# Attention before two MoE layers: the diagonal blocks of P turned in full 128x128 transpositions, the first queries' scores on 128 columns, and POOL's constants moved behind the scan

## The chip, the cores and the metric

One core of a Trainium2 chip runs the whole program. The metric is the device time of one execution in microseconds (us); lower is better. Engines are named as in the profile: PE (TensorE, matrix products; PEld is its weight load), DVE (VectorE), ACT (ScalarE), POOL (GpSimd), SP (SyncE, which here issues the DMAs). L170 is line 170 of the kernel before. A difference of 0.5% of the time (3.7 us) is about what a measurement of this kernel can tell from no change.

## The reference

Causal attention with a forgetting bias over 4 batches, 8 heads, 576 positions and 64 dimensions, then two dense layers on the 2304 x 512 result. The change touches the attention alone.

```python
def _attn_ref(q, k, v, s):                       # q, k, v: (4, 8, 576, 64); s: (4, 8, 576)
    scores = scale * np.matmul(q, k.transpose(0, 1, 3, 2))
    causal = np.triu(np.ones((S, S), dtype=bool), k=1)
    cum = np.cumsum(np.maximum(s, 0.0), axis=-1)
    bias = -(cum[:, :, :, None] - cum[:, :, None, :])
    scores = np.where(causal, -1000000000.0, scores + np.minimum(bias, 0.0))
    ...
    attn = np.exp(scores - max); attn = attn / (sum + 1e-09)
    return np.matmul(attn, v)

def reference(...):
    x = attn_out.transpose(0, 2, 1, 3).reshape(B * S, H * D)
    x = _moe_ref(x)      # (x @ w1) * (x @ w2) @ w3 @ w_out
    return _moe2_ref(x)  # x @ w_in, softmax-gated, layer-normed, @ w_out
```

## The kernel before

**Queries in five tiles.** A head's 576 queries are cut into five tiles `QT`: four of 128 rows that begin at 64, 192, 320 and 448 (tile `i` = 1 to 4, with 64 + 128 i keys: 192, 320, 448, 576), and one of the first 64 queries with 64 keys (`i` = 0). Tiles with the most keys come first. So the last 64 keys of each tile are its diagonal block, of which only the lower 64 queries see anything.

**One head, in stages.** `qk_part` makes the scores on PE: for heads 0 to 7 as full float32 products (L170, two passes each, so that one product is two weight loads and two matmuls in the trace), for heads 8 to 31 as two products of split words (L178 and L179). The tile of 576 keys is written as two halves of 288 columns into two PSUM banks. `softmax_tile` adds the mask and takes the maximum on DVE (L192), and the exponential on ACT (L196), into an SBUF tile `P`, where the five query tiles lie side by side at the offsets `QOF`. `normalise` scales the rows of P (two tiles on ACT at L231, three on DVE at L233).

**Turning P.** The product with V needs P with the keys on the partitions. `tr_part` transposes P on PE in four parts, two heads behind the scores: ten 128x128 blocks (L265), then the five diagonal blocks of 64x64: that of the first queries (L267) and the lower halves of the four others (L274), which come from partitions 64 to 127 of P. Each part has its own PSUM tile `tr`; its columns are copied to `PT` by ACT and DVE in turn (`evict`; L95 on ACT, L97 on DVE), seven copies for a head.

**av.** `av_parts` multiplies PT with V for a pair of heads at once (L298): each head's result takes 64 of the 128 output partitions, so these products are 128x64 in the array, and the two heads' lie beside each other. For head pairs up to head 9 this stands directly behind the second head's transpositions, afterwards one step later, behind those of the next head.

**Fill.** While the batches 1 to 3 are in attention, products of the first dense layer of the batch before (`ab_unit`, L326, names `a` and `b`, 12 products of 288 columns each) are put between the stages. `pump` converts weights that were loaded into `stage` (L363 on ACT, L369 to L374 on DVE). After the attention (345 us) come the rest of the dense layers; the change leaves them alone.

**Order.** The order in which each engine's instructions stand is made by a scheduler when the program is built, from the order in the code and its own estimate of durations. Each engine works through its own in that order.

**Start.** PE runs eight products of zeros (`zp`, L485, 16 matmuls). s is loaded, clipped by DVE (L504) and summed by a scan (L505) into `cum`; DMAs put `cum` into a row of q and of k (`QKN`, L148 and L149), and the first scores follow. POOL writes the constants: zeros and ones for the extra rows of q and k (`aug_rows`), the mask, and zeros for the upper halves of PT and VT (L527 to L532).

## Time and profile before

| what | value |
|---|---|
| median of 3 runs | 738.74 us (738.39 to 741.12) |
| the profiled execution, its own time | 737.73 us |
| its span in the trace | 736.0 us |
| PE busy in the span | 716.7 us |
| DVE, ACT, POOL busy | 504.9, 468.0, 99.5 us |
| attention, from the first scores to the last av | 8.7 to 345 us |

The busy time of PE counts a matmul from its start to its modelled end, so neighbours overlap; the time that one really takes in a row of its kind is the distance from its start to the next one's start. Where PE stands still, the profile shows idle time and what ended it.

### The profile page before, as it was taken

To read this page: it belongs to the slowest core of one execution; us is meant where nothing else is said; L and a number is where in the kernel's file an instruction comes from. 1 tells how busy PE (TensorE), PEld (TensorE's weight loads), DVE (VectorE), ACT (ScalarE), POOL (GpSimd) and SP (SyncE) were. 2 spreads that over 40 slices of the span, in tenths; PEclk is the share of its full clock that TensorE was granted. 3 is DMA by queue.
4 is the path that set the end of the run, shared out by engine and by line. 5 is a ranking of instruction groups with operands and counts; after the bars stand their busy time and mean duration, and the time that the engine had idled before them with its cause. 6 is when DMAs were issued, how large, how long until landed. Compare 5 with 4: busy or idle time off the path is not lost.

```text
span 736.0 us, 13040 instructions
## 1 busy us (share of the span) xinstructions
PE 716.7 (97%) x4682; PEld 625.0 (85%) x4682; DVE 504.9 (69%) x1267; ACT 468.0 (64%) x985; POOL 99.5 (14%) x102
## 2 busy tenths in 40 slices
PE   9889998999999999999998999999999999999997
PEld 6567978888888899899997889988888988888886
DVE  7987978897678888632887876576747365563651
ACT  4987777898766777732544745577646465564652
POOL 5033313142221331000000000001000000000000
PEclk9999999999999999999999999999999999999999
DMA  4644554655476665614566943253234142304221
GB/s 109 186 126 99 174 161 142 194 144 130 127 221 186 182 188 149 208 61 147 170 215 202 355 149 101 58 110 75 79 82 101 44 123 75 89 12 75 44 57 44
DMA packets 79829, 95.52 MB, mean 130 GB/s; under 512 B 41418, under 2 KB 52682, under 8 KB 79764
## 3 DMA queue, kind: packets, MB, share of 16 engines
q1 hardware_dynamic: 79764, 94.69, 45.0%
q8 instruction: 37, 0.61, 0.3%
q14 instruction: 28, 0.23, 0.1%
HBM read 59.04 MB, written 20.14 MB: 108 GB/s over the span
## 4 chain that ended last, share of the span: by engine, by line
PE 73%; DVE 11%; DMA 8%; ACT 5%; issue 2%; POOL 1%; SPq 0%; ACTq 0%; DVEq 0%; POOLq 0%
PE x L721 14%; PE o L847 13%; PE b L326 10%; PE a L326 10%; PE hX L753 5%; DMA stage<-in_w_dram 5%; PE av L298 4%; PE hZ L753 3%; PE tr L265 3%; ACT P L196 2%; PE sc L170 2%; PE sc L178 2%; DVE P L192 2%; DVE stage L374 2%; PE hW L753 2%
## 5 line engine op out<-in xcount | busy, mean ns | idle before, releaser
L196 ACT ACTIVATE P<-P,STAT 128x576 f32<-128x576 f32 (+4 forms) x160 | 88.3, 554 | 31.5 <-DVE STAT L192 30.9
L100 POOL TENSOR_TENSOR QK<-qk,QK 64x1152 fp32r<-64x1152 f32 x24 | 67.1, 2798 | 167.2 <-ACT QK L95 158.9
L721 PE MATMUL x<-gl,MH 128*128 128x256 f32 x288 | 80.4, 280 | 0.0
L721 PE MATMUL x<-gh,ML 128*128 128x256 f32 x288 | 80.2, 279 | 0.0
L721 PE MATMUL x<-gh,MH 128*128 128x256 f32 x288 | 79.9, 280 | 0.0
L192 DVE CUSTOM_DVE_ANT_0 P<-sc,wmask 128x576 f32<-128x576 f32 (+4 forms) x160 | 70.6, 478 | 4.5 <-PE sc L170 3.2
L326 PE MATMUL a<-xT0h,W 128*128 128x288 f32 x256 | 58.1, 300 | 1.9 <-ACT a_sb L338 1.9
L326 PE MATMUL b<-xT0h,W 128*128 128x288 f32 x256 | 57.6, 299 | 1.5 <-DVE STAT L192 0.8
L847 PE MATMUL o<-OH,lh 128*128 128x512 f32 x144 | 57.1, 397 | 0.2 <-DVE ll L100 0.2
L326 PE MATMUL a<-xT1h,W 128*128 128x288 f32 x256 | 57.2, 298 | 0.0
L847 PE MATMUL o<-OH,ll 128*128 128x512 f32 x144 | 57.0, 396 | 0.0
L847 PE MATMUL o<-OL,lh 128*128 128x512 f32 x144 | 57.0, 396 | 0.0
L326 PE MATMUL b<-xT1h,W 128*128 128x288 f32 x256 | 56.5, 295 | 0.0
L721 PEld LDWEIGHTS x<-gl,MH 128*128 128x128 f32 x288 | 54.2, 188 | 1.3
L817 DVE COPY lt<-turned 128x2048 uint16<-128x2048 uint16 x16 | 21.9, 1368 | 48.4 <-DMA turned<-half 48.4
L721 PEld LDWEIGHTS x<-gh,MH 128*128 128x128 f32 x288 | 54.0, 188 | 1.1
L721 PEld LDWEIGHTS x<-gh,ML 128*128 128x128 f32 x288 | 54.1, 188 | 0.9
L346 DVE TENSOR_TENSOR g_sb<-b,a_sb 128x288 f32<-128x288 f32 x64 | 28.8, 449 | 32.8 <-PE b L326 16.7
L363 ACT ACTIVATE stage<-stage 128x512 f32<-128x512 f32 x56 | 36.9, 674 | 21.2 <-DMA stage<-in_w_dram 18.0
L298 PE MATMUL av<-PT,VT 128*64 128x64 f32 (+4 forms) x384 | 50.1, 395 | 0.0
L231 ACT ACTIVATE P<-P,STAT 128x576 f32<-128x576 f32 x64 | 42.7, 717 | 10.4 <-DVE STAT L226 10.4
L338 ACT ACTIVATE a_sb<-a 128x288 f32<-128x288 f32 x64 | 25.6, 401 | 33.3 <-PE a L326 33.1
(193 smaller groups left out, 1965.5 us busy)
## 6 DMA issues: line engine op xcount, KB each, us to landing
stage<-in_w_dram SPq DMA_DIRECT2D x32, 512.0 KB
g_scr<-g_sb SPq DMA_DIRECT2D x32, 288.0 KB
stage<-in_wo_dram SPq DMA_DIRECT2D x16, 512.0 KB
qk<-in_qk_dram SPq DMA_DIRECT2D x24, 288.0 KB
QK<-QK SPq DMA_DIRECT2D x24, 288.0 KB
gl<-g_scr SPq DMA_DIRECT2D x24, 256.0 KB
wf<-wf_scr SPq DMA_DIRECT2D x22, 256.0 KB
out_dram<-o SPq DMA_DIRECT2D x18, 256.0 KB
```

The source lines that it names most:

```text
L100: eng.tensor_tensor(out=dst, in0=src, in1=hi_.bitcast(F32), op=ALU.subtract)
L192: mx = nc.vector.tensor_tensor_reduce(out=dst2, in0=ps_in, in1=msk, scale=-SCALE, scalar=BIG, op0=ALU.add, op1=ALU.min, accum_out=st[0:row ...
L196: ex = nc.scalar.activation(out=dst, in_=dst, func=AF.Exp, bias=st[0:rows, ti:ti + 1], scale=-1.0, accum_out=st[0:rows, 5 + ti:6 + ti],)
L231: nc.scalar.activation(out=dst, in_=dst, func=AF.Copy, scale=r)
L298: nc.tensor.matmul(st["ps"][64 * e:64 * e + 64, 448 + c0:448 + c1], vr[:, j, e], PT[(2 * p + e) % 4][:, o + c0:o + c1], **kw,)
L326: nc.tensor.matmul(ps, w_[:, c, fs], x_[:, c, sl], start=(c == 0 and w_ is WH and x_ is XH), stop=(c == KC - 1 and w_ is WL),)
L338: ab_last[0] = nc.scalar.activation(out=a_sb, in_=ps, func=AF.Copy).ins
L346: ab_last[1] = nc.vector.tensor_tensor(out=g[:, sl], in0=ps, in1=st["a"], op=ALU.mult).ins
L363: nc.scalar.activation(out=high.bitcast(F32), in_=high.bitcast(F32), func=AF.Copy, scale=2.0 ** -112)
L721: last = nc.tensor.matmul(ps[:, a], w_[:, k, m * 128:m * 128 + 128], g_[:, k % 2], start=(k == 0 and w_ is MH and g_ is GH), stop=(k == KF ...
L753: last_h[0] = nc.tensor.matmul(ps, x_[:, k], w_[:, k], start=first and k == 0 and x_ is XH and w_ is WH, stop=k == 1 and x_ is XL, skip_gr ...
L847: nc.tensor.matmul(ps, l_[:, k], w_[:, k], start=(k == 0 and l_ is LH and w_ is OH), stop=(k == KF - 1 and l_ is LL),)
```

## The change

- **P's columns** lie in the order of the tiles 2, 3, 1, 4, 0, and the tile of 576 keys has its last 64 keys in front (its scores are one product of 512 columns and one of 64, in place of two of 288). So a window of 128 columns that begins with the diagonal block of tile 2, 3 or 1 ends in the first 64 columns of the next tile.
- **Transpositions**: the five of 64x64 are replaced by three of 128x128 on such windows. The first queries' normalised block is written by `normalise` into the masked upper half of tile 1's diagonal block, and the diagonal block of tile 4 lies behind it: one transposition turns these three (with tile 1's own) at once. All thirteen of a head are now of one shape.
- **Copies to PT**: six for a head in place of seven; the last two are one of 64 partitions x 3 x 64 on DVE and one of 128x128 on ACT. DVE and ACT now take the same ones for every head. The last one holds the first queries' block, from which the first product of av is made.
- **First queries' scores** use 128 columns of q as the stationary side in place of 64 (the upper 64 rows of the result are not read).
- **V's last 64 rows** lie on partitions 64 to 127 in place of 0 to 63.
- **Constants**: a second mask `lmask` for the tile of 576 keys; the scan's zeros are `wmask`; ACT writes the ones (`const_rows`), DVE the zeros of head 1's extra rows; POOL's constants for STAT, PT and VT are issued behind the mask's diagonal, which waits for the scan.

```diff
-    QT = []
-    off = 0
-    for i in range(4, 0, -1):
-        QT.append((64 + 128 * (i - 1), 128, 64 + 128 * i, off))
-        off += 64 + 128 * i
...
+    QOF = {}
+    PW = 0
+    for i in (2, 3, 1, 4, 0):
+        QOF[i] = PW
+        PW += 64 + 128 * i
+    QT = [(64 + 128 * (i - 1), 128, 64 + 128 * i, QOF[i]) for i in range(4, 0, -1)] + [(0, 64, 64, QOF[0])]
...
     def qk_mm(h, ps_view, ti):
-        q0, rows, n, _ = QT[ti]
+        q0 = QT[ti][0]
+        rows = 128
...
         if part == 0:
-            ps = bigtile("sc")
-            qk_mm(h, [(0, ps[:, 0, 0:HS]), (HS, ps[:, 1, 0:HS])], 0)
-            softmax_tile(h, 0, ps[:, :, 0:HS], cut=2)
+            ps = flat(bigtile("sc"))
+            qk_mm(h, [(0, ps[:, 512:1024]), (512, ps[:, 448:512])], 0)
+            softmax_tile(h, 0, ps[:, 448:1024])
             return
...
         for ti, (q0, rows, n, o) in enumerate(QT):
-            dst = p_t[h][0:rows, o:o + n]
+            src = dst = p_t[h][0:rows, o:o + n]
+            if ti == 4:
+                dst = p_t[h][0:rows, QOF[1] + 128:QOF[1] + 192]
...
+    WINS = (
+        [QOF[i] for i in (1, 2, 3)] + [QOF[4] + 64],
+        [QOF[2] + 128, QOF[3] + 128, QOF[4] + 192, QOF[4] + 448],
+        [QOF[3] + 256, QOF[4] + 320],
+        [QOF[2] + 256, QOF[3] + 384, QOF[1] + 128],
+    )
...
-        if part == 2:
-            nc.tensor.transpose(ps[0:64, 256:320], pt[0:64, QOF[0]:QOF[0] + 64], ident[0:64, 0:64])
...
-            for i in range(1, 5):
-                last_tr[0] = nc.tensor.transpose(
-                    ps[0:64, 64 * i:64 * i + 64],
-                    pt[64:128, QOF[i] + 128 * i:QOF[i] + 128 * i + 64],
-                    ident[64:128, 64:128],
-                )
-            for j in (1, 3):
-                src = ps[0:64, 64 * j:64 * j + 128].rearrange("p (a b) -> p a b", a=2)
-                evict(lambda t: half_view(t, j), src)
+        for n, o in enumerate(WINS[part]):
+            last_tr[0] = nc.tensor.transpose(ps[:, 128 * n:128 * n + 128], pt[:, o:o + 128], ident)
...
+            thirds = [x.rearrange("p (a b) -> p a b", b=w) for x, w in ((PT_[0:64, 0:960], 320), (ps[0:64, 0:384], 128))]
+            evict(thirds[0][:, :, 0:64], thirds[1][:, :, 64:128])
+            evict(PT_[:, H0:H0 + 128], ps[:, 256:384])
             p_t.pop(h)
...
         def mm(j, c0, c1, **kw):
-            o = KO[j] - 128 * j
+            o = KO[j] - 128 * j if c1 > 64 else H0
...
-    nc.gpsimd.memset(zero, 0.0)
+    nc.gpsimd.memset(wmask, 0.0)
...
-    for i in range(2):
-        aug_rows(QN[i], KN[i])
+    for i, eng in enumerate((nc.gpsimd, nc.vector)):
+        eng.memset(QN[i][0:64], 0.0)
+        eng.memset(KN[i][0:64], 0.0)
+        const_rows(QN[i], KN[i])
+    nc.gpsimd.memset(lmask, 0.0)
     nc.vector.tensor_scalar(out=s_sb, in0=s_sb, scalar1=0.0, scalar2=1.0 / SCALE, op0=ALU.max, op1=ALU.mult)
-    nc.vector.tensor_tensor_scan(out=cum, data0=s_sb, data1=zero, initial=0.0, op0=ALU.add, op1=ALU.add)
+    nc.vector.tensor_tensor_scan(out=cum, data0=s_sb, data1=wmask[0:NH], initial=0.0, op0=ALU.add, op1=ALU.add)
...
+    behind_scan = tc.issue_after(diagonal.ins)
+    behind_scan.__enter__()
     for st in STAT:
         nc.gpsimd.memset(st, 1.0)
     for t in PT:
-        for j in range(5):
+        for j in (2, 3, 1):
             nc.gpsimd.memset(t[64:128, KO[j]:KO[j] + 64], 0.0)
```

**On PE, in the attention of the later heads.** Here the transpositions of one head (`tr`) stand between fill products (`b`, L326) and the scores of another head's tile of 576 keys (`sc`). Before:

```order
L326 MATMUL b<-xT0h,W_124 128x288
L265 MATMUL tr<-ident,P 128x128 x10
L267 MATMUL tr<-ident,P 64x64
L274 MATMUL tr<-ident,P 64x64 x4
L178 MATMUL sc<-QK_615 128x288
L179 MATMUL sc<-QK_615 128x288
L178 MATMUL sc<-QK_615 128x288
L179 MATMUL sc<-QK_615 128x288
```

and in the changed kernel:

```order
L303 MATMUL b<-xT0h,W_125 128x288
L247 MATMUL tr<-ident,P 128x128 x13
L177 MATMUL sc<-QK_595 128x512
L178 MATMUL sc<-QK_595 128x512
L177 MATMUL sc<-QK_595 128x64
L178 MATMUL sc<-QK_595 128x64
L303 MATMUL a<-xT0h,W_122 128x288
```

Fifteen transpositions of two shapes have become thirteen of one, and the four score products of 288 columns are two of 512 and two of 64. Every other head's transpositions are followed by av in place of scores, before as after. Over the whole program av stands on PE in 24 unbroken runs before and in 20 now. Of the 32 heads' small transpositions before, 10 had av directly behind them; now av stands 17 times directly behind a transposition of 128x128, where it did so 7 times.

**On PE, the scores of the four smaller tiles of a later head.** Before:

```order
L178 MATMUL sc<-QK_679 128x448
L179 MATMUL sc<-QK_679 128x448
L178 MATMUL sc<-QK_679 64x64
L179 MATMUL sc<-QK_679 64x64
L178 MATMUL sc<-QK_679 128x320
L179 MATMUL sc<-QK_679 128x320
L178 MATMUL sc<-QK_679 128x192
```

and now:

```order
L177 MATMUL sc<-QK_595 128x448
L178 MATMUL sc<-QK_595 128x448
L177 MATMUL sc<-QK_595 128x64
L178 MATMUL sc<-QK_595 128x64
L177 MATMUL sc<-QK_595 128x320
L178 MATMUL sc<-QK_595 128x320
L177 MATMUL sc<-QK_595 128x192
```

The order is the same; the two products of the first queries write 128 rows in place of 64.

**On POOL, at the start**, up to the constants of PT (`s_zero` holds s and the scan's zeros, `QKN` q and k with their extra rows). Before:

```order
masks.py:199 AFFINE_SELECT ident<-ident 128x128
L521 MEMSET wmask 128x576
L497 MEMSET QKN_110 64x576
L498 MEMSET QKN_110 64x576
L527 MEMSET STAT_115 128x16
...
L530 MEMSET PT_111 64x64 x4
L499 MEMSET QKN_109 2x576
L500 MEMSET QKN_109 2x576
L530 MEMSET PT_111 64x64
L522 AFFINE_SELECT wmask<-wmask 128x128
```

and now:

```order
masks.py:199 AFFINE_SELECT ident<-ident 128x128
L489 MEMSET lmask 128x576
L506 AFFINE_SELECT wmask<-wmask 128x128
L515 MEMSET STAT_116 128x16
...
L518 MEMSET PT_112 64x64 x3
```

Between the identity and the mask's diagonal, which now waits for the scan, one memset of 128x576 is left.

## Rows read from the trace of the kernel before

**Rows 1.** Page, chain that ended last: shares of the span by engine.

```profile
PE 73%; DVE 11%; DMA 8%; ACT 5%; issue 2%; POOL 1%; SPq 0%; ACTq 0%; DVEq 0%; POOLq 0%
```

**Rows 2.** Windows of the attention: length, then busy time (and count) by engine.

```profile
core 0: us, PE busy (x) PEld busy (x) DVE busy (x) ACT busy (x) POOL busy (x), PEclk, DMA share, GB/s
9.00:66.00 57.00, 51.94 (x308) 34.99 (x308) 47.60 (x172) 48.00 (x136) 11.32 (x28) 1.00 0.52 140
66.00:158.00 92.00, 86.99 (x658) 77.59 (x654) 79.08 (x228) 75.64 (x185) 25.94 (x9) 1.00 0.55 161
158.00:285.00 127.00, 126.72 (x996) 114.09 (x996) 100.29 (x297) 96.46 (x245) 33.32 (x13) 1.00 0.62 176
285.00:345.00 60.00, 58.80 (x463) 52.75 (x462) 29.40 (x83) 30.23 (x77) 2.55 (x1) 1.00 0.34 107
```

**Rows 3.** Chain that ended last, 9 to 66 us: shares by line.

```profile
by line: PE sc L170 26.0%; PE av L298 17.8%; ACT P L196 16.4%; PE tr L265 10.4%; ACT P L231 5.9%; ACT QK L95 4.1%; ACT PT L95 3.3%; DVE P L192 2.5%; issue 2.2%; PE sc L178 1.8%; DVE W L100 1.7%; PE tr L274 1.5%; PE sc L179 1.4%; DVE P L233 
```

**Rows 4.** Timeline and chain of the start: start us, length us, what.

```profile
1.24 7.19 PE L485 MATMUL zp<-zz 128*128 128x288 f32 x16 [1.24 <-DVE zz L482]
2.66 2.00 DVE L504 TENSOR_SCALAR s_zero<-s_zero 32x576 f32<-32x576 f32 x1 [1.47 <-DMA s_zero<-in_s_dram]
4.78 1.34 DVE L505 TENSOR_TENSOR_SCAN cum<-s_zero 32x576 f32<-32x576 f32 x1
6.86 1.67 DMA QKN<-cum
8.66 0.48 PE L170 MATMUL sc<-QKN 128*128 128x288 f32 x1 [0.23 <-DMA QKN<-cum]
```

**Rows 5.** Timeline of PE: one head's transpositions, scores of another behind them.

```profile
219.69 1.25 PE L265 MATMUL tr<-ident,P 128*128 128x128 f32 x10
220.88 0.24 PE L267 MATMUL tr<-ident,P 64*64 64x64 f32 x1
220.88 0.41 PE L274 MATMUL tr<-ident,P 64*64 64x64 f32 x4
221.22 0.40 PE L178 MATMUL sc<-QK 128*128 128x288 f32 x1
221.46 0.29 PE L179 MATMUL sc<-QK 128*128 128x288 f32 x1
```

**Rows 6.** Timeline of PE: transpositions with av behind them, in two places.

```profile
207.23 1.26 PE L265 MATMUL tr<-ident,P 128*128 128x128 f32 x10
...
208.75 0.28 PE L298 MATMUL av<-PT,VT 128*64 128x64 f32 x2
...
24.93 0.49 PE L265 MATMUL tr<-ident,P 128*128 128x128 f32 x3
25.35 0.27 PE L298 MATMUL av<-PT,VT 128*64 128x64 f32 x1
```

**Rows 7.** Timeline of PE: scores of the later heads.

```profile
215.11 0.37 PE L179 MATMUL sc<-QK 128*128 128x448 f32 x1
215.32 0.19 PE L178 MATMUL sc<-QK 128*64 128x64 f32 x1
215.63 0.31 PE L179 MATMUL sc<-QK 128*128 128x320 f32 x1
215.78 0.25 PE L178 MATMUL sc<-QK 128*128 128x192 f32 x1
215.98 0.32 PE L178 MATMUL sc<-QK 128*128 128x288 f32 x1
216.53 0.29 PE L326 MATMUL a<-xT1h,W 128*128 128x288 f32 x1
```

**Rows 8.** Timeline of PE: scores of the first heads, in float32.

```profile
14.82 3.21 PE L170 MATMUL sc<-qk 128*128 128x288 f32 x12
...
17.86 0.49 PE L265 MATMUL tr<-ident,P 128*128 128x128 f32 x3
18.19 1.14 PE L170 MATMUL sc<-QKN 128*128 128x288 f32 x4
19.16 0.27 PE L265 MATMUL tr<-ident,P 128*128 128x128 f32 x1
```

**Rows 9.** Groups of DVE by form: count, busy us, mean ns, idle before.

```profile
L97 DVE COPY PT<-tr 64x64 f32<-64x64 f32 x16 | 3.3, 206 | 1.2 <-ACT PT L95 1.2
```

**Rows 10.** Waits of PE, 9 to 158 us: us in total, times, longest.

```profile
PE tr L265 <- ACT PT L95: 1.1, 1, 1.1
```

More of the change, by code (lines that the diff above doesn't have):

```diff
@@ L108, in tile_attention_moe @@
     wmask = at.tile([128, S], F32, name="wmask")
+    lmask = at.tile([128, S], F32, name="lmask")
     QK = {}
-    KO = [0]
-    for j in range(5):
-        KO.append(KO[-1] + S - 128 * j)
+    KO = {2: 0, 3: 320, 4: 576, 1: 640, 0: 1024}
+    H0 = 512
     QKN = [at.tile([128, 4, S], F32, tag="QK", bufs=2, name=f"QKN{i}") for i in range(2)]
@@ L116, in tile_attention_moe @@
     KN = [t[:, 1] for t in QKN]
-    PT = [at.tile([128, KO[5]], F32, name=f"PT{i}") for i in range(4)]
+    PT = [at.tile([128, 1600], F32, name=f"PT{i}") for i in range(4)]
     STAT = [at.tile([128, 16], F32, name=f"STAT{i}") for i in range(PB)]
@@ L143, in load_v @@
         )
-        nc.sync.dma_start(out=vr[0:64, 4].rearrange("p e d -> p (e d)"), in_=vE[b, hp])
+        nc.sync.dma_start(out=vr[64:128, 4].rearrange("p e d -> p (e d)"), in_=vE[b, hp])
     def load_aug(h, src):
@@ L185, in softmax_tile @@
         dst = pt[0:rows, o:o + n]
-        msk = wmask[0:rows, S - n:S] if rows == 128 else wmask[0:rows, S - 128:S - 64]
-        if cut:
-            dst2 = dst.rearrange("p (a b) -> p a b", a=cut)
-            msk = msk.rearrange("p (a b) -> p a b", a=cut)
-        else:
-            dst2 = dst
+        msk = lmask if ti == 0 else wmask[:, S - n:S] if rows == 128 else wmask[0:rows, S - 128:S - 64]
         mx = nc.vector.tensor_tensor_reduce(
-            out=dst2, in0=ps_in, in1=msk, scale=-SCALE, scalar=BIG,
+            out=dst, in0=ps_in, in1=msk, scale=-SCALE, scalar=BIG,
             op0=ALU.add, op1=ALU.min, accum_out=st[0:rows, ti:ti + 1],
@@ L215, in qk_part @@
             q0, rows, n, _ = QT[ti]
-            view = ps[0:rows, o:o + n]
-            qk_mm(h, [(0, view)], ti)
-            views.append((ti, view))
+            qk_mm(h, [(0, ps[:, o:o + n])], ti)
+            views.append((ti, ps[0:rows, o:o + n]))
             o += n
@@ L512, in tile_attention_moe @@
     nc.vector.memset(qk3[0:64], 0.0)
-    nc.vector.memset(qk3[0:2, 0], 1.0)
-    nc.vector.memset(qk3[32:34, 1], -1.0)
+    const_rows(QN[2], KN[2])
     load_head(2)
@@ L520, in tile_attention_moe @@
     nc.sync.dma_start(out=cum_scr.bitcast(F32), in_=CK.bitcast(F32))
-    nc.gpsimd.memset(wmask, 0.0)
-    nc.gpsimd.affine_select(
+    diagonal = nc.gpsimd.affine_select(
         out=wmask[:, S - 128:S], in_=wmask[:, S - 128:S], pattern=[[-1, 128]],
@@ L528, in tile_attention_moe @@
     for t in PT:
-        for j in range(5):
+        for j in (2, 3, 1):
             nc.gpsimd.memset(t[64:128, KO[j]:KO[j] + 64], 0.0)
     for t in VT:
-        nc.gpsimd.memset(t[64:128, 4], 0.0)
+        nc.gpsimd.memset(t[0:64, 4], 0.0)
+    behind_scan.__exit__(None, None, None)
     nc.sync.dma_start(out=gln, in_=g_ln.rearrange("(k p) -> p k", p=128))
```

47 lines of the change are left out of this document (17 added, 30 removed).

## The prediction

> **What bounds the kernel now.** I read the chain that ended last first: PE holds 73% of the span [rows 1], so what counts is the time that PE's instructions take from start to start, and where PE stands still. The windows of the attention show the second: PE is busy for all but 5.1 us of 9 to 66, 5.0 us of 66 to 158, 0.3 us of 158 to 285 and 1.2 us of 285 to 345 [rows 2]. So there are two kinds of stretches. From 158 us on PE alone sets the end, and each nanosecond that PE gains or loses there counts in full. Before 158 us DVE and ACT are busy for 82 to 86% too, and in 9 to 66 the lines of PE hold some 59% of the chain (26.0 + 17.8 + 10.4 and the three small ones), ACT most of the rest [rows 3]. There PE's gains count in part: I take 60%.
>
> **The change part by part.** Starts are used for durations, since a matmul's shown length overlaps the next one's.
>
> *Transpositions.* A 128x128 one takes (1.25 - 0.27)/9 = 0.109 us from start to start (ten in 1.25 [rows 5], one alone 0.27 [rows 8]). Where scores follow, the fifteen take from 219.69 to 221.22, and the first score product behind them takes 0.24 to its successor [rows 5] in place of (216.53 - 215.98)/4 = 0.137 [rows 7]; that is 1.53 + 0.10 = 1.63. Only 10 x 0.109 + 5 x 0.06 = 1.39 of it is work by the steps within each kind ((0.41 - 0.24)/3 = 0.06 for a small one); the remaining 0.24 lies where the shape changes. Thirteen of one shape are 13 x 0.109 = 1.42: 0.21 less. Where av follows, the fifteen take 208.75 - 207.23 = 1.52 [rows 6]. av is of another shape itself, so the change of shape stays: from the third full transposition (24.93 + 2 x 0.109 = 25.15) to av directly behind it at 25.35 is 0.20 [rows 6]. Then 12 x 0.109 + 0.20 = 1.51, which is 0.01 less. By the order, 22 heads are of the first kind and 10 of the second: -4.7 us. av also stands in 4 runs fewer; entering costs 0.20 - 0.11 = 0.09 and leaving up to 0.2, so up to 1.2 us more, of which I take half. Sum -5.3 us (bounds -4.7 and -5.9). Of this, 5.75 pairs of heads at 0.22 lie in 158 to 285 (-1.3), six heads in 285 to 345 (-0.9), and -3.1 before 158 us, about -2.0 of it in 9 to 66, where av is broken up most.
>
> *Scores of heads 0 to 7* (float32). The tile of 576 keys takes 19.16 - 18.19 = 0.97 for four passes of 288 columns [rows 8], 0.84 ns a column. Two passes of 512 are 0.86, and two of 64 columns can't be faster than their weight loads of 128 columns, 0.109 each as in the transpositions: 1.08, or +0.11. The other four tiles take 17.86 - 14.82 - 0.97 = 2.07 [rows 8]; their 960 columns in two passes are 1.62 of it, and 0.45 goes to the two passes of the 64x64 product and the change of shape around them. With 128 columns of q there is no other shape, and 0.22 is left: -0.23. Net -0.12 for each of 8 heads, -1.0 us.
>
> *Scores of heads 8 to 31* (split words). Four products of 288 take 0.55 [rows 7]. Now there are two of 512, 0.21 x 512/448 = 0.24 each after the one of 448 [rows 7], and two of 64 columns with a full weight load, which the trace doesn't hold. From above, two full loads, 0.22; from below, one load hidden behind the 512, 0.11. The nearest row is that of the two products of 192, 0.20 [rows 7], which are also shorter than a weight load; I take 0.20. So 0.68 in place of 0.55, +0.13. In the first queries' tile the pair of 64x64 and the first product of 320 take 215.63 - 215.32 = 0.31, with a change of shape in it; now 0.20 + 0.15 = 0.35, +0.04. Net +0.17 for each of 24 heads, +4.1 us (bounds: -0.01 and +0.21 a head, -0.2 to +5.0 us). By stretches that is 8, 12 and 4 heads: +1.4, +2.0, +0.7. So PE's sum is -1.0 - 2.0 = -3.0 in 9 to 66, +0.3 in 66 to 158, +0.7 in 158 to 285 and -0.2 in 285 to 345.
>
> *The start.* The first scores waited for the DMA of `cum`, which landed at 8.53 [rows 4] and is issued when the scan is through, 6.12. The scan waited for L504, which took 2.00 us, longer than the scan itself (1.34) over the same 32x576 [rows 4], while POOL was writing constants. In the changed order POOL has one memset left there. If L504 then ends a microsecond earlier, PE gains less than that: the last of the 16 products of zeros starts at 1.24 + 7.19 - 0.41 = 8.02 and takes 0.24, so the scores start at 8.27 at the earliest in place of 8.66. Bounds 0 and -0.4; I take -0.4, since 2.00 us is out of line with the scan. The Trainium skill (SBUF — State Buffer, section Who interferes with whom) says that VectorE in its two-port mode and GpSimd take a shared pair of ports one at a time, and that the second blocks for a whole instruction. By that rule L504 ends soon after the last early memset, and the term is -0.4; without it the term may be 0, and the sum 0.4 higher.
>
> *Copies, masks, constants.* One copy to PT fewer for each head, the shortest of which takes 0.21 on DVE [rows 9], shared by DVE and ACT: 0.1 us per head each at most. It counts only where these engines are on the chain, 16 heads before 158 us at 40%: -0.3 (bounds 0 and -0.6). The ones on ACT and the zeros on DVE at the start cost nothing: both engines wait for the scan's input or the first scores there (DVE idle 1.47 before L504 [rows 4]). Without that cover, or if DVE's two memsets outlast its 1.47 us, the scan comes as much later, and PE has only the 0.4 us to lose before its first scores do too. The SP queue gets no DMA more; the offset of V's last rows costs nothing.
>
> *Sum.* -0.4 (start) - 3.0 x 60% = -1.8 (9 to 66) + 0.2 (66 to 158, of +0.3) + 0.7 - 0.2 - 0.3 = -1.8 us. The profiled execution took 737.73, 1.0 less than the median; it would come to 735.9. Against the median, 738.74 - 1.8 = 736.9; I say 736.7, as two of the three runs before and the profiled one lie at the lower end.
>
> **The rivals.**
>
> 1. *PE's gain counts in full, and some idle time goes.* PE is idle for 10 us before 158 us [rows 2], behind ACT and DVE. With one shape of transposition the order has fewer broken runs. If all of -3.0 counts and 2 us of the idle time go: 738.74 - 0.4 - 3.0 + 0.3 + 0.5 - 0.6 - 2.0 = 733.5. For it: 59% of the chain in 9 to 66 is PE's already. Against it: ACT is busy for 48 of 57 us there.
> 2. *The gain is lost.* ACT, DVE and the weights' DMAs keep the pace before 158 us, and the start gives nothing, since the scan's input or the DMA is what is late. Then +0.5 us of PE's later stretches and some of the copies are left: 738.9.
> 3. *av waits for the last copy.* av's first product reads the first queries' block, which is now in the head's last copy, always on ACT. For heads 0 to 9 av stands directly behind the transpositions. If ACT is late by 1.1 us as once before [rows 10], five pairs cost 5.5 us: 742.2, slower. It decides from 0.4 us a pair. Against it: one such wait in 149 us, and the scheduler can put other products between.
> 4. *The small shapes were cheap.* If the gaps around the 64x64 transpositions were not the shapes' doing, five at 0.06 would be traded for three at 0.109: +0.03 for each of 32 heads, and no gain from shapes in the scores of heads 0 to 7. The sum is then +1.0 + 4.1 + 0.9 - 0.7 = +5.3, 744. The gaps in two places speak against it [rows 5, 6]. The Trainium skill (TensorEngine Tiling, section Theoretical Speedup) gives small matrices up to twice the rate in small tiles, which is this rival; its section Key Properties says that a change of tiling mode drains the engine, and by that the trace agrees.
>
> **How the numbers follow.** Forecast 0.52 (735 to 738.3), rival 1 0.23, rival 2 0.17, rival 3 0.05, rival 4 0.03. The time is the forecast's, 736.7. The range, 733.2 to 739.6, takes in rivals 1 and 2 for the most part; below it lies the part of rival 1 in which more idle time goes, about 0.1, above it rivals 3 and 4. The bounds of the scores alone (-4.3 and +0.9) and of the start (+0.4) stay within it. 0.5% of 738.74 is 3.7 us, so faster means below 735.0: rival 1 and a few of the forecast's, 0.27. Slower means above 742.4: 0.06. The same: 0.67.
>
> **What the profile will show.** Thirteen transpositions at 0.109 and the next fill or score product without the 0.24; two products of 64 columns taking 0.20 together in the split scores; the first scores at 8.3; L490 well under 2 us; a period of two heads after 158 us longer by 0.1 us, and the attention's first 66 us shorter by some 2 us. If the pair of 64 takes 0.1, the steady stretch is shorter than before and I am too high by 4 us; if the first stretch's idle time grows by as much as PE saves, I am too low by 2.

## The result, and the profile after

The changed kernel took 731.75 us (median of 6 runs, 730.61 to 732.8) against 739.3 us (6 runs, 738.39 to 741.12): a ratio of 0.9897, 95% interval 0.9875 to 0.992. That is 7.6 us or 1.03% faster, and below the range. The profiled execution of after took 732.8 us, the highest of its six, that of before 737.73, the lowest of its six. So the two traces differ by 4.9 us only, and 2.6 us of the difference between the medians is in neither trace.

The chain that ended last, shares of the span by engine [rows 1]:

```profile
PE 81%; DVE 9%; DMA 5%; ACT 2%; issue 2%; SPq 0%; DVEq 0%; ACTq 0%
```

The windows of the attention [rows 2]:

```profile
core 0: us, PE busy (x) PEld busy (x) DVE busy (x) ACT busy (x) POOL busy (x), PEclk, DMA share, GB/s
9.00:66.00 57.00, 53.53 (x333) 40.24 (x332) 50.23 (x179) 53.45 (x147) 12.31 (x11) 1.00 0.56 149
66.00:158.00 92.00, 86.66 (x622) 79.80 (x620) 79.77 (x219) 73.16 (x179) 23.65 (x8) 0.96 0.56 163
158.00:285.00 127.00, 127.00 (x969) 116.06 (x969) 100.23 (x284) 94.70 (x233) 34.45 (x13) 1.00 0.60 171
285.00:345.00 60.00, 60.00 (x463) 55.03 (x462) 29.49 (x82) 28.77 (x71) 0.15 (x1) 1.00 0.36 129
```

PE's idle time fell from 5.1 to 3.5 us in 9 to 66 and from 1.2 to 0 in 285 to 345; in 66 to 158 it is 5.3 in place of 5.0, and the granted clock is 0.96 in place of 1.00.

A window of fixed times holds more work in the faster kernel. So I compared the starts of the same piece of work in the two traces (a and b are the products of the fill):

| work that starts | before, us | after, us | difference | gained since the row above |
|---|---|---|---|---|
| first scores | 8.66 | 7.14 | -1.52 | -1.52 |
| av of heads 6 and 7 | 62.87 | 56.92 | -5.95 | -4.43 |
| 361st product of a and b | 162.03 | 158.50 | -3.53 | +2.42 |
| 865th product of a and b | 282.77 | 280.45 | -2.32 | +1.21 |
| 1153rd product of a and b | 342.52 | 338.60 | -3.92 | -1.60 |
| 33rd product of m, the first stage behind the attention | 404.72 | 399.39 | -5.33 | -1.41 |
| 145th product of x, the next one | 459.78 | 454.84 | -4.94 | +0.39 |

Nearly 6 us are won in the first 60 us, and 2.4 of them are lost again before 158.

The start, as a timeline [rows 4]:

```profile
1.24 6.06 PE L462 MATMUL zp<-zz 128*128 128x288 f32 x16 [1.24 <-DVE zz L459]
2.61 0.50 DVE L490 TENSOR_SCALAR s_sb<-s_sb 32x576 f32<-32x576 f32 x1 [0.22 <-DMA s_sb<-in_s_dram]
3.22 1.35 DVE L491 TENSOR_TENSOR_SCAN cum<-s_sb,wmask 32x576 f32<-32x576 f32 x1
5.30 0.59 SPq L147 DMA_DIRECT2D QKN<-cum  x1
7.14 2.03 PE L169 MATMUL sc<-QKN 128*128 128x512 f32 x6
```

L490 takes 0.50 in place of 2.00, and the scan is through 1.5 us earlier. The products of zeros end 1.1 earlier too (7.30 for 8.43), which the prediction had taken as fixed.

PE in the steady stretch, a head's transpositions and the scores of another behind them [rows 5, 7]; the first row is the last ten of thirteen:

```profile
216.83 1.25 PE L247 MATMUL tr<-ident,P 128*128 128x128 f32 x10
217.84 0.48 PE L177 MATMUL sc<-QK 128*128 128x512 f32 x1
218.16 0.39 PE L178 MATMUL sc<-QK 128*128 128x512 f32 x1
218.38 0.19 PE L177 MATMUL sc<-QK 128*128 128x64 f32 x1
218.41 0.27 PE L178 MATMUL sc<-QK 128*128 128x64 f32 x1
218.64 0.40 PE L303 MATMUL a<-xT1h,W 128*128 128x288 f32 x1
```

The thirteenth transposition starts at 216.83 + 9 x 0.109 = 217.81, and the scores follow it without the 0.2 of a changed shape. But the two products of 64 columns hold PE from 218.38 to 218.64. A period of two heads (865th less 577th product of a and b, over three) went from 22.08 to 22.40 us.

### The profile page after: what moved, and what is told of

Same layout as the page of the kernel before. It is cut to its first block, busy times and chain, and to the rows that moved or that the text cites. A ratio compares the mean times of both kernels' runs of the same rounds, so it can differ in the third digit from the quotient of the medians.

```text
span 731.1 us, 12896 instructions
## 1 busy us (share of the span) xinstructions
PE 714.2 (98%) x4618; PEld 631.5 (86%) x4618; DVE 507.7 (69%) x1251; ACT 470.4 (64%) x977; POOL 95.2 (13%) x88
## 4 chain that ended last, share of the span: by engine, by line
PE 81%; DVE 9%; DMA 5%; ACT 2%; issue 2%; SPq 0%; DVEq 0%; ACTq 0%
PE x L710 14%; PE o L836 14%; PE a L303 12%; PE b L303 11%; PE av L275 6%; PE hX L742 5%; PE tr L247 5%; DMA stage<-in_w_dram 4%; PE hZ L742 3%; PE sc L178 2%; PE sc L177 2%; PE hW L742 2%; PE hY L742 2%; DVE stage L351 2%; PE sc L169 1%
## 5 line engine op out<-in xcount | busy, mean ns | idle before, releaser
L190 ACT ACTIVATE P<-P,STAT 64x64 f32<-64x64 f32 (+4 forms) x160 | 88.5, 556 | 22.9 <-DVE STAT L186 22.3
L247 PE MATMUL tr<-ident,P 128*128 128x128 f32 x416 | 54.4, 275 | 3.5 <-DVE STAT L186 2.7
L247 PEld LDWEIGHTS tr<-ident,P 128*128 128x128 f32 x416 | 46.8, 141 | 5.4 <-issue 1.6
L226 ACT ACTIVATE P<-P,STAT 128x576 f32<-128x576 f32 x64 | 42.7, 717 | 10.5 <-DVE STAT L219 10.4
```

Source lines behind the costliest of these rows:

```text
L190: ex = nc.scalar.activation(out=dst, in_=dst, func=AF.Exp, bias=st[0:rows, ti:ti + 1], scale=-1.0, accum_out=st[0:rows, 5 + ti:6 + ti],)
L226: nc.scalar.activation(out=dst, in_=src, func=AF.Copy, scale=r)
L247: last_tr[0] = nc.tensor.transpose(ps[:, 128 * n:128 * n + 128], pt[:, o:o + 128], ident)
```

## The experiments

Theory A: PE's work before 158 us counts in full, and with the earlier start and less idle time it makes the 7.6 us. The rivals are in the expectations. Ratios are to runs of the kernel before taken beside each one on the same chip. Differences to the changed kernel are differences of medians that were taken at different times, between which the median of before moved by up to 1.0 us.

**1. The kernel before, again.** No edit.

> The kernel before, unchanged, profiled once more. Theory A (the 7.5 us come from PE's work in the first 158 us counting in full, from the earlier start and from less idle time): its time is that of before, 738.4 to 741.1, and the milestones of its profile repeat those of the first profile of before to 0.3 us (fill product 36 some 6.6 us later than in the changed kernel's). Theory B (the milestones differ because stretches of half granted clock fall where they please): the 3.4 us of half clock that stand at 396 us in the first profile stand elsewhere or are gone, and the milestones shift by 1.5 to 2 us with them.

738.79 us (12 runs), ratio 1.0001 (0.9983 to 1.002). Its profile repeats the first one's starts to 0.00 us up to 43 us; then it is up to 1.4 us late at heads 4 and 5, and 1.0 late from 158 us on. Half-clock stretches of 3.4 us (granted clock 0.50, the lower of its two levels, 1.2 and 2.4 GHz) stand at 53, 125 and 398 us; in the first profile only the one at 397 us (and in both one in the last microseconds). So two executions of one program differ by 1 us and more behind 43 us, and a difference of that size there says nothing by itself.

**2. The start alone, and the change without it.**

The first is the kernel before with the new start (POOL's constants behind the scan, `const_rows` on ACT, head 1's zeros on DVE, `wmask` as the scan's zeros), the second the changed kernel with POOL's constants where they stood before (`wmask` stays the scan's zeros):

```diff
-    for i, eng in enumerate((nc.gpsimd, nc.vector)):
...
+    for i in range(2):
+        aug_rows(QN[i], KN[i])
...
-    behind_scan = tc.issue_after(diagonal.ins)
```

> The kernel before with the new start alone (POOL's constants behind the scan, rows of ones on ACT, zeros of two heads on DVE). Theory A: the first scores come at 7.2 in place of 8.7, and all of it counts: 1.5 us less than before, about 737.8. Rival (as predicted): the first scores gain 0.4, and 60% or all of it counts: 738.9 to 739.1. Rival (start and clock alone made the change): most of the 7.5 us, 733 or less.

> The changed kernel with the start of before. Theory A: first scores at 8.7 again, 1.5 us more than the changed kernel, 733.2. Rival (the wait is taken up by idle time before 158 us): 0.6 us or less more, 732.3. Rival (the start made the change): near 738.

738.72 us (ratio 0.9992, 0.9973 to 1.0011) and 732.2 us (0.9904, 0.9886 to 0.9922). What was L504 took 0.5 us in both, even in the second, whose POOL memsets are not behind the scan:

```profile
2.61 0.50 DVE L488 TENSOR_SCALAR s_sb<-s_sb 32x576 f32<-32x576 f32 x1 [1.42 <-DMA s_sb<-in_s_dram]
2.76 0.87 POOL L487 MEMSET lmask<- 128x576 f32 x1
3.57 0.57 POOL L473 MEMSET QKN<- 64x576 f32 x1
```

In before, DVE's instruction began at 2.66 and ended at 4.66, while POOL ran memset behind memset from 2.76 to 4.78; here it began at 2.61, and POOL's memset is the one that took longer. So in this profile the scan was free although POOL's constants had not moved. It is one profile, and the two engines begin within 0.15 us of each other. In all four profiles with the whole start of before (two of them come below) DVE was held to 4.7; in the fifteen with the new start it was held in three, to 3.6, by the one memset that is left there. So the new order limits what a lost meeting costs; that it was needed for a free scan is not shown. First scores came at 7.71 and 7.11. In the start alone a second thing decides, the time at which the clock rises under the products of zeros (their distance falls from 0.48 to 0.24 us at 7.4 us in before, at 5.2 in after, 5.1 in the repeat of before, 6.3 in the start alone). The record of the granted clock begins with this rise; in the windows PEclk says 1.00 for the time ahead of it as well, and only the distance tells the lower level there. The gain of 0.96 of the start alone stood to 76 us in its trace, was a loss of 0.3 at 138 us, and 1.0 at the end; in the medians nothing of it can be told. The start is worth 0 to 1.5 us, and is not the change.

**3. The old transpositions and copies in the changed kernel.**

```diff
-        [QOF[2] + 256, QOF[3] + 384, QOF[1] + 128],
+        [],
...
+            nc.tensor.transpose(ps[0:64, 256:320], pt[0:64, QOF[0]:QOF[0] + 64], ident[0:64, 0:64])
```

> The changed kernel with the transpositions and copies of before (ten of 128x128 and five of 64x64 for each head, seven copies); scores and start as in the changed one. Theory A (PE's time counts in full everywhere): 5.3 us for the transpositions (0.21 for each head followed by full-width work) and up to 1 us of idle time: 737 to 738. My prediction's share of 60% before 158 us: 3.1 x 0.6 + 1.3 + 0.9 = 4.1, less 0.3 of copies: 735.5 to 736. Rival 4 (small shapes cheap): no more than the changed kernel, 731 to 732.

744.37 us, ratio 1.0064 (1.0041 to 1.0087): 12.6 more than the changed kernel, and 5.1 more than before. No theory had that. In the steady stretch its period is 22.49 us: so there the new transpositions give 0.09 for two heads and not the 0.22 of the prediction, and the new scores cost 0.41 (0.20 a head). The rows show where most of the rest of the 0.22 goes:

```profile
227.96 0.41 PE L257 MATMUL tr<-ident,P 64*64 64x64 f32 x4
228.30 0.50 PE L177 MATMUL sc<-QK 128*128 128x512 f32 x1
228.90 0.27 PE L178 MATMUL sc<-QK 128*128 128x64 f32 x1
229.01 0.38 PE L309 MATMUL a<-xT1h,W 128*128 128x288 f32 x1
```

Here the fill follows 0.11 behind the last score; in the changed kernel, where the transpositions are shorter, it follows 0.22 behind. The rest lies before the steady stretch: this kernel is 6.1 us later than the changed one at the 25th fill product and 9.7 at the 361st. It also has seven copies, so that ACT and DVE change turns from head to head, and experiments 4 and 5 put that alone at 8.7 us: the 12.6 is not the price of the transpositions.

**4. More work on PE alone; one copy more; the first queries on 64 columns.**

More work on PE for heads 0 to 7, whose results nothing reads:

```diff
+            for n in (2, 3, 2, 3):
+                nc.tensor.transpose(ps[:, 128 * n:128 * n + 128], pt[:, 0:128], ident)
```

Seven copies:

```diff
-            evict(thirds[0][:, :, 0:64], thirds[1][:, :, 64:128])
+            evict(thirds[0][:, 0:2, 0:64], thirds[1][:, 0:2, 64:128])
+            evict(thirds[0][:, 2:3, 0:64], thirds[1][:, 2:3, 64:128])
```

First queries:

```diff
-        q0 = QT[ti][0]
-        rows = 128
+        q0, rows = QT[ti][:2]
```

> The changed kernel with four further 128x128 transpositions, whose results nothing reads, for each of heads 0 to 7: 8 x 4 x 0.109 = 3.5 us more for PE before 66 us, and nothing more for the other engines. Theory A (PE's time counts in full there): 3.5 us more than the changed kernel, 735.2. My prediction's share of 60%: 2.1 us more, 733.9. Rival (ACT and DVE keep the pace, and the gain came from their copies): less than 1 us more, below 732.8. Rival (idle time grows along with PE's work, as it fell with it): 5 us or more, above 736.7.

> The changed kernel with its copy of three 64x64 blocks cut into one of two and one of one, so that each head has seven copies, as before, and ACT and DVE take turns from head to head; PE's instructions are the same. Theory A (PE's time): no more than 0.3 us more than the changed kernel, 732. Rival (a copy fewer on ACT and DVE is what saved the time before 158 us, where both are busy): 2 to 4 us more, 734 to 736.

> The changed kernel with the first queries' scores on 64 columns of q again, as before, and all else as changed. My prediction's terms: 0.23 us more for each of heads 0 to 7 (1.8 us, in full by theory A, 1.1 at 60%), and 0.04 less for each of 24 heads (0.9): 0.2 to 0.9 us more than the changed kernel, 732.0 to 732.7. Rival (a 64x64 product is cheap beside 128x128 ones): 1 us or more less than the changed kernel, below 731.

742.22 us (ratio 1.0053, 1.0029 to 1.0078), 740.5 (1.0021, 1.0003 to 1.004) and 736.47 (0.9962, 0.9943 to 0.9982): 10.5, 8.7 and 4.7 us more than the changed kernel, far above what each adds. Theory A falls as an addition of terms. In the first of them the 3.5 us of PE work, with a start 1.0 later, are 3.7 us at the 25th fill product: so behind the first scores, in one profile of each, PE's time counted for (3.7 - 1.0) / 3.5 = 77%, near the 60% that I had taken. The surplus comes later: it is 2.1 us late at 137 us and 8.2 at 160. In the second, PE has the same work as in the changed kernel, in another order from 26 us on, and is 0.9 us late at the first scores, 3.6 at 69 us, 9.4 at 168. The third's profiled execution took 734.29 and ends 1.4 us behind the changed kernel's, so most of its 4.7 stands in no trace. The second's chain in 9 to 66 us lies on ACT for 55% (29.4, 12.4, 7.4, 4.1 and 2.0):

```profile
by line: ACT P L190 29.4%; ACT P L226 12.4%; PE sc L169 8.4%; ACT PT L93 7.4%; PE av L276 5.9%; DVE stage L352 5.4%; DVE P L186 4.8%; ACT QK L93 4.1%; PE tr L247 3.5%; issue 3.2%; DVE P L228 2.5%; ACT stage L341 2.0%; PE sc L177 1.7%; PE a 
```

In the changed kernel, by the part of the row that is shown, for 16% [rows 3]:

```profile
by line: PE sc L169 13.6%; ACT P L190 12.5%; PE tr L247 11.3%; PE av L275 10.9%; DVE P L186 8.9%; DVE PT L95 6.6%; DVE P L228 5.1%; DVE stage L351 5.1%; ACT P L226 3.9%; DVE xT0l L98 3.5%; issue 3.3%; DVE stage L347 3.2%; DVE STAT L218 2.8%
```

**5. Which engine has which copy.** Three arrangements of the changed kernel's copies, one with seven, and two of the seven copies of before.

Seven copies with the second piece always on DVE; then all six exchanged; the first pair, and the last pair, exchanged:

```diff
+            hi(thirds[0][:, 2:3, 0:64], thirds[1][:, 2:3, 64:128], V)
...
-    PCOPY = [None, V]
+    PCOPY = [V, None]
...
+            hi(dst, src, (None, V, V, None, V, None)[(cnt[0] - 1) % 6])
+            hi(dst, src, (V, None, V, None, None, V)[(cnt[0] - 1) % 6])
```

And the kernel before with every head alike, the last copy on DVE, or on ACT:

```diff
+            cnt[0] = 0
...
+            hi(dst(PT_), src, (V, None, V, None, V, V, None)[(cnt[0] - 1) % 7])
```

> The changed kernel with the seven copies of the run before, but the cut copy's second piece always on DVE, beside the first, so that ACT and DVE keep the same copies in every head. Theory C (an odd number of copies makes ACT and DVE change turns from head to head, and in every second head ACT, which has the exponentials, gets the copy of 512 columns): within 1.5 us of the changed kernel, 731.5 to 733.3. Rival N (one copy more, whoever has it): about as slow as the seven in turns, 738 to 741. Rival D (any small change of the order loses a round of the weights between 100 and 158 us): 736 or more, with the step at 130 to 150 us and not before 66.

> The changed kernel with its six copies, ACT and DVE exchanged: ACT gets those of 512, 128 and 192 columns in every head, DVE those of 384, 256 and 128. Theory C (ACT is the late one before 66 us, so it matters which copies it has): 2 to 6 us more than the changed kernel, 734 to 738. Rival N: no more than 1 us beside it.

> The changed kernel with one pair of its copies exchanged: ACT gets the one of 512 columns, DVE the one of 384; the others stay. Theory F (ACT must not have the 512): 736 to 741. Theory L (the last copy, which av waits for, must not be on DVE): within 1.5 us of the changed kernel, 731 to 733.3.

> The changed kernel with another pair of copies exchanged: DVE gets the last one (128x128, the first queries' keys, which av reads first), ACT the one of three 64x64 blocks before it. Theory L: 736 to 741, with waits of av or of the scores for DVE's copies. Theory F: within 1.5 us of the changed kernel, 731 to 733.3.

> The kernel before with its seven copies, but every head beginning with DVE, so that the copies do not change engines from head to head. Theory C: 2 to 5 us less than before, 734 to 737, with ACT's share of the chain in 9 to 66 us lower. Rival N (the number of copies): as before, 738 to 740.

> The kernel before with the same engine for each of its seven copies in every head, 512, 128, 64 and the first pair of 64x64 on DVE, 384, 256 and the last pair on ACT, as the changed kernel has them. If the arrangement of the copies is what the change gained most by: 733 to 735.5. If the transpositions' own time and the idle time that goes with it made it: 738 to 740. By theory L it is in any case 4 us or more below the fixed arrangement that ended on DVE, 742.5.

| copies | median, us | ratio to before, interval |
|---|---|---|
| changed kernel: DVE 512, 128, 3 x 64; ACT 384, 256, last 128 | 731.75 | 0.9897 (0.9875 to 0.992) |
| seven, engines as in the changed kernel | 732.8 | 0.9915 (0.989 to 0.9939) |
| seven, in turns from head to head | 740.5 | 1.0021 (1.0003 to 1.004) |
| six, all exchanged | 740.95 | 1.0015 (0.9994 to 1.0035) |
| six, the 512 on ACT, the 384 on DVE | 739.86 | 0.9998 (0.9977 to 1.0019) |
| six, the last on DVE, 3 x 64 on ACT | 737.69 | 0.9972 (0.9953 to 0.9991) |
| before: seven, in turns | 739.3 | 1 |
| before, every head alike, last on DVE | 742.54 | 1.0039 (1.0015 to 1.0063) |
| before, every head alike, last on ACT | 743.87 | 1.0061 (1.0038 to 1.0085) |

One more copy in itself costs 1 us or nothing (rival N falls); giving the copies to other engines costs up to 9. That is the price of the engines together with what the scheduler makes of them: by tile names and shapes, PE's order in the traces is that of the changed kernel only in its repeat, in the changed kernel with the old start and, behind the zeros, in the late start of experiment 7. Of its 4618 matmuls some 35 stand elsewhere in the seven with fixed engines, 102 in the seven in turns, 43 with all six exchanged, 123 with the 512 on ACT, 38 with the last on DVE. As 35 go with 1 us, 38 with 6 and 43 with 9, the number that moved does not tell the time. With all exchanged and with the last on DVE PE's order is the changed kernel's to 35 us; up to there they lose 0.4 and 0.1 us to it, the start left out, and the repeat, with the same order throughout, loses 0.3. So what the engines cost shows only where the order differs too, and the runs do not tell the two apart. Theory F and theory L are both right in part: either exchange costs 6 to 8 us, nearly as much as all three together. But theory C's counterpart in before failed: the same arrangement there is 4.6 us slower. One piece is seen in rows. In six kernels where ACT has the copy of 512 columns, in all heads or in every second one, PE waits at some 311 us for ACT. These are PE's waits in 285 to 345 us (total, times, longest), of before and of the changed kernel with the 512 on ACT; the changed kernel has none there:

```profile
PE a L326 <- ACT a_sb L338: 1.2, 1, 1.2
```

```profile
PE a L303 <- ACT a_sb L315: 1.9, 2, 1.5
```

It is there, with 1.0 to 1.9 us, in before, its repeat, the start alone, the old transpositions, all exchanged and the 512 on ACT. It is in none of the kernels whose heads all have the 512 on DVE, nor in the seven in turns, which wait 0.3 for DVE. What PE waits for is not the copy of 512 itself. In before, with all exchanged and with the 512 on ACT, ACT stood for 1.1 to 1.4 us for weights to convert, with the copy of `a` behind that in its queue. These are ACT's rows of before:

```profile
309.93 0.68 ACT L363 ACTIVATE stage<-stage 128x512 f32<-128x512 f32 x1 [1.33 <-DMA stage<-in_wo_dram]
310.50 0.41 ACT L338 ACTIVATE a_sb<-a 128x288 f32<-128x288 f32 x1
```

It makes 1.2 of the -1.60 of the table above.

The two kernels before with fixed copies have half-clock stretches at 23 and at 61 us in their profiles, which neither profile of before has there. From the first scores to 23.1 us the first of them does what before did, to 0.01 us, PE's 1.5 us of idle time in 19 to 23.2 included, and yet its clock fell to 0.50 there and that of before did not. So part of what these two profiles lose is no effect of the edit; their medians, of 12 runs each, are slower all the same.

**6. Keys in another order, and POOL's subtraction on DVE.** The last 64 keys of heads 8 to 31 are loaded in front, so that the tile of 576 keys is two products of 288 for each word again.

```diff
+        nc.sync.dma_start(out=qk2[64:128, 1, 64:S], in_=qkT[b, hh, :, 1, 0:512])
+        after[0] = nc.sync.dma_start(out=qk2[64:128, 1, 0:64], in_=qkT[b, hh, :, 1, 512:S])
...
+                qk_mm(h, [(-64, ps[:, 0, 0:HS]), (HS - 64, ps[:, 1, 0:HS])], 0)
```

In a second kernel with these keys, and a third one without, DVE has the subtraction of heads 8 to 19:

```diff
-        lo(t[64:128, 1::2], raw, t[64:128, 0::2], G)
+        lo(t[64:128, 1::2], raw, t[64:128, 0::2], V if h < 20 else G)
```

> The changed kernel with the keys of heads 8 to 31 loaded in the order 512 to 575, 0 to 511 (three DMAs more for each of these heads), so that their tile of 576 keys is two products of 288 for each word again and not one of 512 and one of 64. By the steady stretch of the two traces, 512 and 64 cost 0.22 to 0.25 us more a head than the two of 288: 24 heads give 5 to 6 us, 726 to 727, if PE's time counts in full. Rival (the DMAs more on SP's queue, or the smaller rows that they move, hold the heads or the weights up): the gain is lost, 731 or more.

> The kernel with rotated keys, with the low words of q and k of heads 8 to 19 subtracted on DVE and not on POOL. Theory P (DVE's instructions that meet POOL's subtraction of 2.7 us take up to 3.0 us in place of 0.6, and each makes PE wait for weights by 2 to 3 us): these waits, 2.2, 2.7 and 2.8 us at 82, 96 and 121 us, go; 3 to 6 us less than with the keys alone, 725 to 728. Rival (DVE is busy for 86% there already, and some 0.7 to 1.3 us more for each of 12 heads makes it the bound): 730 or more.

> The changed kernel with the low words of q and k of heads 8 to 19 subtracted on DVE and not on POOL. Theory P (what is left of PE's waits between 66 and 158 us, 5.3 us in the changed kernel's profile, is DVE meeting POOL's subtraction): 2 us or more less, below 729.8. Rival (DVE's own work takes the place of the meetings): 731 to 733.

730.5 us (ratio 0.9887, 0.9862 to 0.9912), 729.54 (0.9877, 0.9845 to 0.9909) and, with the subtraction alone, 733.78 (0.992, 0.9891 to 0.9948). The keys do what was expected in the steady stretch: 21.95 us for two heads, 0.44 less than the changed kernel, and 0.13 less than before. But 2.7 us are lost to the changed kernel between 65 and 161 us. The rows of DVE and POOL at one of three such places there:

```profile
77.38 5.89 POOL L98 TENSOR_TENSOR QK<-qk,QK 64x1152 fp32r<-64x1152 f32 x2 [13.59 <-ACT QK L93]
80.69 3.13 DVE L362 SCALAR_TENSOR_TENSOR stage<-stage 128x512 uint32<-128x512 uint32 x1
```

L362 converts weights, and takes 0.69 where POOL is idle. With POOL's subtraction on DVE (1.35 us each) no DVE instruction in 66 to 158 is stretched any more, and PE's idle time there falls from 8.3 to 5.3 us, with the clock back at 1.00 (columns as above, first with the subtraction on POOL):

```profile
66.00:158.00 92.00, 83.68 (x601) 77.49 (x600) 83.25 (x217) 71.24 (x172) 23.28 (x8) 0.94 0.52 156
```

```profile
66.00:158.00 92.00, 86.73 (x654) 79.95 (x650) 83.11 (x236) 76.89 (x188) 0.00 (x0) 1.00 0.57 169
```

Theory P is shown as a mechanism. As a gain it is not: with the keys in front the medians differ by 1.0 us, and the changed kernel is 2.0 slower with the subtraction on DVE, with intervals that overlap both times. What gives the gain back is not shown. In both profiles with the subtraction on DVE the loss lies before 66 us: the 25th fill product comes 4.1 and 2.8 us later (0.9 and 1.1 of it the start's), with stretches of half clock at 52 us (6.8 and 3.4 us long) that the kernels without it do not have in theirs. And in the changed kernel PE's idle time in 66 to 158 stays at 5.5 us, though no DVE instruction is stretched. The kernel with both is the fastest of this study by its median, but its interval and that of the changed kernel overlap.

**7. A shift of everything, and the changed kernel again.**

```diff
-    for i in range(8):
+    for i in range(12):
         nc.tensor.matmul(zp[:, 0:HS], zz[:, 0:128], zz, start=True, stop=True)
```

> The changed kernel with 24 in place of 16 products of zeros ahead of the first scores, which nothing reads: 8 x 0.243 = 1.9 us later first scores (9.1 for 7.1), every instruction behind them in the same order. Theory A (what the start gives counts in full): 1.9 us more than the changed kernel, 733.7. Theory S (a shift is taken up by waits for the weights, which come at their own pace): 0 to 1 us more, below 732.8. Theory K (the stretch before 158 us answers to a shift by more than the shift, through longer waits and half-clock stretches behind them): 735 or more.

> The changed kernel, unchanged: 730.6 to 732.8 as in its first six runs. If half-clock stretches between 90 and 130 us belong to its order of work they stand at 94 and 125 us again; if they come by chance, elsewhere or fewer.

734.55 us (ratio 0.9938, 0.9922 to 0.9954) and 730.95 (5 runs, 730.14 to 735.68; ratio 0.9885, 0.9863 to 0.9908). The shift of 1.5 us in its profile (the clock rose at another time) is 2.0 at 60 us, gone for a while at 129 to 137 us (-0.3), and 1.9 in the last stage. By the medians it costs 2.8 us against the first runs of the changed kernel and 3.6 against the repeat taken beside it, where 1.9 were worked out. So it counts in full or by more; S falls, and K, whose bound of 735 it just misses, is neither shown nor excluded. The repeat tells more. Its profiled execution took 735.68, 2.9 more than the first profile of the same program, while its other four took 730.1 to 731.2. Up to 90 us it runs 0.5 to 0.8 behind the first; at the start its L490 was held to 3.6 us. DVE and POOL then, in the first profile and in the repeat:

```profile
93.97 3.93 POOL L98 TENSOR_TENSOR QK<-qk,QK 64x1152 fp32r<-64x1152 f32 x1 [11.41 <-ACT QK L93]
94.11 0.67 DVE L347 SCALAR_TENSOR_TENSOR stage<-stage 128x512 uint32<-128x512 uint32 x1
```

```profile
94.66 2.67 POOL L98 TENSOR_TENSOR QK<-qk,QK 64x1152 fp32r<-64x1152 f32 x1 [12.00 <-ACT QK L93]
94.80 3.08 DVE L347 SCALAR_TENSOR_TENSOR stage<-stage 128x512 uint32<-128x512 uint32 x1
```

Each time DVE's instruction is recorded 0.14 behind POOL's. In one, POOL takes 3.93 and this DVE instruction is not held, nor the next of 0.6 (a later one, which begins at 96.95, takes 1.51); in the other POOL takes its 2.67 and DVE is held to its end. Behind it PE waits 2.6 us for a product of the fill (total, times, longest):

```profile
PE b L303 <- DVE STAT L186: 2.6, 1, 2.6
```

The repeat is 2.5 us behind at the 169th fill product, and at the 361st too. The Trainium skill (SBUF — State Buffer, section Who interferes with whom) says that whoever issues first has the shared ports for its whole instruction, and that the other blocks; the trace agrees in that one waits for the other's whole instruction, and shows that the same program falls on either side. Who issued first the recorded starts do not tell, as POOL's is 0.14 ahead both times.

## Why the prediction was wrong

**What failed is the step that counted 60% of PE's gain in 9 to 66 us, left idle time as it was, and put which engine has which copy at nothing.** -1.8 was counted there; the traces show -4.43 between the first scores and av of heads 6 and 7, as much as all of PE's 3.0 and 1.4 more. That is rival 1 (0.23, 733.5), which had idle time go as well, and which missed the result by 1.8. The share for PE's work alone was not bad: 77% in experiment 4. What both left out is what the copies do to the idle time.

**The copies were put at -0.3, bounds 0 and -0.6.** I priced them by their busy time. Experiment 5 shows that with the same work on PE their engines, and the order that goes with them, move the time by 1 to 9 us. That DVE and ACT take the same copies in every head was told of the change, and given no price. Rows 3 already had ACT on the chain for 30% of 9 to 66 us; a copy of 512 columns ahead of the next exponential would be late work on that chain, which is an argument and no measurement.

**The start was bounded by a row that is not fixed.** -0.4 was taken since the products of zeros leave PE at 8.27; the clock rose earlier and they left it at 7.14, which makes -1.52 in the trace. That was chance: it rose as early in the repeat of before. Its first half, L504 well under 2 us, was right; the reason, POOL's constants, is not shown, as L504's successor was as short with them in place (experiment 2).

**66 to 158 was not read.** The prediction carried +0.3 of PE's through it. I had looked at its windows, not its chain. Here it is, of before:

```profile
by line: DMA stage<-in_w_dram 23.6%; DVE P L192 11.0%; DVE W L100 10.5%; DVE stage L374 8.5%; DVE stage L370 6.9%; DVE P L233 5.8%; DVE PT L97 4.7%; issue 4.4%; ACT P L196 4.0%; PE a L326 3.8%; PE b L326 3.7%; ACT QK L95 2.5%; DVE stage L36
```

And of after:

```profile
by line: DMA stage<-in_w_dram 18.3%; PE a L303 12.5%; PE b L303 11.0%; PE av L275 9.3%; PE tr L247 7.7%; DVE W L98 6.1%; PE sc L178 4.8%; PE sc L177 4.7%; DVE P L186 4.4%; issue 4.3%; DVE stage L351 4.2%; DVE stage L347 2.7%; DVE PT L95 2.3
```

It is bound by weights on their way from the DMA through DVE, and by whether DVE meets POOL there. Where it does, PE can stand for 2 to 3 us behind it: it does at three places of the kernel with the keys in front, where eight DVE instructions take 1.6 to 3.1 us. The granted clock can fall to 0.50 for 3.4 us behind a wait: in the profile of after it did so behind waits of 1.4 and 2.1 us, in the repeat behind 2.6 and not behind another 2.1. In the profile of after, just before and in one of these stretches:

```profile
121.60:124.60 3.00, 0.91 (x7) 0.90 (x7) 3.00 (x7) 1.66 (x6) 0.90 (x1) 1.00 0.31 68
124.60:128.00 3.40, 3.40 (x17) 3.40 (x16) 3.40 (x15) 3.38 (x9) 0.00 (x0) 0.50 0.90 258
```

**The 2.6 us in neither trace.** One such stretch lowers the mean granted clock of an execution by 3.4 x 0.5 / 735 = 0.0023. The 35 runs of before beside the first experiments have a mean of 0.993, so some 3.0 of them; the 11 of the changed kernel 0.997, so 1.2. At up to 1.7 us each that is an estimate of up to 3 us. The profile of after has two of them between 90 and 130 us, that of before none.

**Mis-sized, off the main step:** the transpositions gained 0.09 for two heads in the steady stretch where 0.22 was counted, and the new scores cost 0.20 a head where 0.17 was. The table has +1.21 in 158 to 283 us, where +0.7 was counted for 158 to 285.

**Rightly predicted:** thirteen transpositions at 0.109, no gap of a changed shape, L490 under 2 us, the steady stretch longer (0.31 for two heads in place of 0.12). The two products of 64 columns, put at 0.20, take 0.14 and delay the product behind them by 0.08 (0.214 in place of 0.131), and where transpositions stand ahead by more (0.25 and 0.24). Rivals 2 to 4 did not come; av does not wait for the last copy.

**Open:** the surplus can't be shared out among the parts. Taking away one part costs 0.4 (start), 4.7 (128 columns) or 12.6 us (transpositions and copies), and their sum is more than double the gain. The last two also change the scheduler's order (PE's from 9 and from 18 us on), and before 158 us that alone may be worth several us; an edit that changes the order and no work was not tried. Why the fixed copies slow the kernel before is not settled either.

## What to carry to other kernels

In a stretch where three engines are busy for over 80%, work on the bounding engine was here the smaller part of an edit's effect. Ask which engine gets each small copy and what stands behind it in that queue, look at what the scheduler reorders with it, and give it a range as wide as the stretch's idle time, both ways. Read the chain of every stretch that an argument passes through, not its busy shares alone. Profile a kernel twice before explaining 2 us of it.

## What the runs showed of the hardware

- DVE and POOL: the same DVE instruction took 0.67 or 3.08 us in two executions of one program, 0.14 us behind the start of a POOL subtraction in both; POOL's took 3.93 or 2.67. At the start DVE was held for 2.00 in place of 0.50 us while POOL ran memset behind memset, and for 0.92 in the repeat of the changed kernel, where POOL ran one.
- The granted clock rose at 4.2 to 7.5 us in twenty profiles that had done the same on PE up to then (products of zeros from 1.24 us on).
- Two profiles that agreed to 0.01 us from the first scores to 23.1 us (before, and before with every head alike and the last copy on DVE) parted there: in one the granted clock fell to 0.50 for 3.4 us, in the other it stayed.
- Of two passes of 64 columns with 128 columns of weights, the first was followed after 0.03 us and the second after 0.11, and the product behind them took 0.214 to its successor in place of 0.131; with thirteen transpositions just ahead it was 0.03, 0.22 and 0.24.
